# Moving the K products of a state-space gradient kernel behind the next chunk's Z groups, and a fourth staging buffer in its last dense block

## The chip, the cores and the metric

The kernel runs on one core of one Trainium2 chip. It is one launch: inputs and outputs lie in the device's main memory, and the time is that of the launch on the device, in microseconds (us). Five engines work side by side, each with its own queue of instructions that it takes in order: PE (TensorE, matrix products and transposes), DVE (VectorE, elementwise), ACT (ScalarE, copies and functions), POOL (GpSimd) and SP (SyncE), the last two used here almost only to issue DMAs. ACT issues DMAs too. A profile names a wait by the engine that ended it.

## The reference

The kernel computes a forward pass and all its gradients. The forward mixes two branches of the same input x (2048 positions, 448 channels) by a gate per position; branch a is a diagonal state-space convolution with 256 states per channel, branch b a dense layer with squared ReLU.

```python
def _A_ref(u, A_re, A_im, B_re, B_im, C_re, C_im, log_dt, Dskip):
    dt = jnp.exp(log_dt)[:, None]
    A = A_re + 1j * A_im
    Bc = B_re + 1j * B_im
    Cc = C_re + 1j * C_im
    logdA = dt * A
    dB = dt * Bc
    l = (lambda x, dt: x.astype(dt))(jnp.arange(L), A_re.dtype)
    P = jnp.exp(logdA[:, :, None] * l[None, None, :])
    K = jnp.einsum("dn,dnl,dn->dl", Cc, P, dB).real
    ...
    Yf = Uf * Kf[None, :, :, :]                    # convolution of u with K by FFT
    y = irfft2(Yf)[:, :, 0, :L]
    return y.transpose(0, 2, 1) + u * Dskip[None, None, :]

def _B_ref(x, w1, b1, w2, b2):
    h = jnp.einsum("bsd,df->bsf", x, w1) + b1
    r = jnp.where(h > 0, h, 0)
    return jnp.einsum("bsf,fd->bsd", r * r, w2) + b2

g = _sigmoid((x * gate_w).sum(-1, keepdims=True))
out = g * a + (1 - g) * b
_out, _vjp = jax.vjp(_f, ...)                      # then the gradients of all inputs
```

The positions l are rounded to the inputs' type, so that above 256 several positions share one value: the convolution kernel K needs only some of its rows.

## The kernel before

The work has four stretches. First inputs are loaded, their transforms are made (fwd1, fwd2) and powers of the roots exp(dt A) are stored in rec_d. Then comes the **chunk loop** over 14 chunks of 32 channels, with the **dense stages** of branch b beside it. Then the row of K values is read back as xs and transformed, multiplied with the stored spectra (product), and turned back (inv1, inv2). Last come the weight gradients (grad_w2, grad_w1, lines 1218 to 1254).

*The chunk loop.* A chunk c needs two tables per state and channel: X, with 13 of the powers at coarse steps, and Y, with 64 at fine steps. DVE builds them by repeated doubling: x_pair makes the X tables of two chunks at even c (step_x, lines 762 to 767), build_y makes a chunk's Y table in two halves (double, lines 774, 775, 777). ACT supplies the roots for it: expand_x (lines 804, 805) and expand_y (lines 809, 811). From the tables follow:

- kgen(c), line 841: the K values of the chunk, 128 small matmuls (64 x 16 each) of Y with X into the PSUM bank X; k_out (line 849) copies them out, and for chunks 9 and 13 stores the K rows gathered since the last store to k_d (line 855);
- tables_t, lines 867 and 868: X turned by PE, also through bank X, copied by ACT;
- load_yt, line 887: Y turned by a DMA on SP; for the last of four groups turn_yt does it by PE and ACT (lines 879, 880), through bank X;
- back_z(c-1), lines 910 and 914: a Z group is 32 small matmuls of turned Y with the gradient rows dk, into bank F; ACT copies it. Groups 0 and 1 make z01, groups 2 and 3 z23;
- back_p(c-1), lines 930 and 939: DVE multiplies Z with the turned X (called P here, two instructions of 2048 columns per half), and PE sums the products with the matrix sel;
- dk_chunk, lines 892 and 893: ACT lays out the gradient rows.

In the source, iteration c makes back_z and back_p of chunk c-1 around the build of chunk c; kgen(c) stands behind the second half of build_y(c). Y lies in two buffers by the parity of c.

*The dense stages.* hidden (608, 611, ACT 613 and 615) makes the ReLU of a block of 512 positions; project (matmuls 1080, copy 1081, store to br_d 1082) makes 128-position tiles of the dense output, and with w = 1 of the gradient with respect to x; row_block (matmuls 1143 and 1146, ACT 1148, DVE 1155, store 1156) makes the gradient of the hidden values from r, which ACT loads (1129). row_block(3) is the last block and stands behind fwd1 of the K transform in the source. project takes its staging buffers br in turn, three of them, one per tile of the block.

*What sets the order.* The source's order isn't that of the engines. When the program is built, the framework's scheduler fixes each engine's queue by dependencies, buffers and its own estimate, so that the matmuls of the dense stages stand in PE's queue between those of the chunk loop, and the dense product 1155 between DVE's doublings. An issue_after makes one instruction stand behind another. A PSUM bank is reused when the last reader has released it; bank X is shared by kgen, tables_t and turn_yt.

*After the loop.* xs is filled from k_d by 18 DMAs: 11 from SP and 7 from ACT (line 1172, alternating by the first column of a run of equal positions; and line 1175). PE transforms it in fwd1 (line 231, evacuated in lines 208 and 209), the result goes through gd to fwd2 (line 259). grad_w2 then loads rT_d (line 1218) into the memory that held the weights of project, and turns it (line 1223).

Of the kernel before, what the change touches and what calls it, by code (L numbers as in the profile page):

```python
# [338 lines left out]
def kernel(ctx, tc, A_u, A_A_re, A_A_im, A_B_re, A_B_im, A_C_re, A_C_im, A_log_dt, A_Dskip,  # L339
# [487 lines left out]
                              PIY[:, k, ws].rearrange("p w t d -> p (w t) d"), rows=rows)  # L827
        return last

    def kgen(c):  # L830
        ps = K.ps("X", [P, 16 * NA])
        for i in range(CW):
            for gg in range(2):
                for jt in range(2):
                    g = 2 * jt + gg
                    ch = 8 * gg + i
                    k = 0
                    for h in range(2):
                        w = g * 16 + h * 8 + i
                        for t in range(2):  # L840
                            T_.matmul(ps[64 * jt:64 * jt + 64, ch * NA:ch * NA + NA], lhsT=Ys[c % 2][:, w, t, :], rhs=XWs[c % 2][:, 1 - t, w, :, 1],  # L841
                                      start=(k == 0), stop=(k == 3), tile_position=(0, 64 * jt))
                            k += 1
        return ps

    def k_out(c, ps):
        cp, cc = c // GC, c % GC
        kv = KS[:, :, cp].rearrange("p a (g q i) -> p q a g i", g=2, q=GC)[:, cc]
        S.copy(kv, ps[:].rearrange("p (g i a) -> p a g i", g=2, a=NA)[:, 0:VA])
        if c in (9, NCH - 1):  # L850
            c0, c1 = (0, 5) if c == 9 else (5, 7)
            for jt in range(2):
                for (a0, na, st_) in ((0, 2, 1), (2, 2, 2), (4, 2, 1), (6, 6, 256), (12, 1, 1)):
                    nb_ = 1 if a0 == 12 else 64
                    (nc.scalar if jt and c > 9 else G_).dma_start(bass.AP(tensor=k_d, offset=AOFF[a0] * D + 224 * jt + 32 * c0, ap=[[4 * D, nb_], [st_ * D, na], [1, 32 * (c1 - c0)]]),
                                 KS[64 * jt:64 * jt + nb_, a0:a0 + na, c0:c1].rearrange("p a c e -> p a (c e)"))

    def tables_t(c, gp):
        nonlocal xi
        XT = XTr[xi % 4].rearrange("p (t g n) -> p t g n", g=2, t=2)  # L860
        xi += 1
        pt = K.ps("X", [P, 4, 256], bf16)
        for t in range(2):
            for gg in range(2):
                for h in range(2):
                    w = (2 * gp + gg) * 16 + h * 8
                    T_.transpose(pt[:, 2 * t + gg, h * P:(h + 1) * P], XWs[c % 2][:, t, w:w + 8, :, 0].rearrange("p w a -> p (w a)"), ident[:])
        S.copy(XT.rearrange("p t g n -> p (t g n)"), pt[:].rearrange("p a n -> p (a n)"))  # L868
        return XT
# [22 lines left out]
        S.copy(DKs[:, c % 2, 0, :, :, 0:VA], src)  # L892
        S.activation(DKs[:, c % 2, 1, :, :, 0:VA], src, ACT.Copy, scale=brow[:, 0:1])

    def back_z(c, YTs, gs):

        nonlocal zi
        cc = c % GC
        DKc = DKs[:, c % 2]
        zb = Zr[zi % 2].rearrange("p (s t g n) -> p s t g n", t=2, s=2, g=2)  # L900
        zi += 1
        for gg, g in enumerate(gs):
            psz = K.psF()
            for s in range(2):
                for par in (1, 0):
                    for ii in range(4):
                        i = 2 * ii + par
                        m = (1 + par) * NA
                        for t in range(2):
                            T_.matmul(psz[32 * ii:32 * ii + m, t, 256 * s:256 * s + 256],  # L910
                                      lhsT=DKc[64 * t:64 * t + 64, s, g, 2 * ii:2 * ii + 1 + par].rearrange("p i a -> p (i a)"),
                                      rhs=YTs[g][64 * t:64 * t + 64, :, i, :], start=True, stop=True, tile_position=(64 * t, 32 * ii),
                                      skip_group_check=True)
            S.copy(zb[:, :, :, gg].rearrange("p s t n -> p t s n"), psz[:].rearrange("p t (s n) -> p t s n", s=2))  # L914
        return zb

    def back_p(c, XT, zb, gs, after):
# [102 lines left out]
    for c in range(NCH + 1):  # L1020
        z01 = z23 = None
        if c == 0:
            x_next(0)
        elif c % 2 == 1 and c < NCH:
            XTs[c] = [tables_t(c, 0)]
        if 0 < c < NCH:
            YTs[c] = []
        if c > 0:
            z01 = back_z(c - 1, YTs[c - 1], (0, 1))
        if c % 2 == 1 and c < NCH:  # L1030
            XTs[c].append(tables_t(c, 1))
        if c > 0:
            z23 = back_z(c - 1, YTs[c - 1], (2, 3))
        ap = None
        for half in range(2):
            if c < NCH:
                if c > 0:
                    ay = build_y(c, half, ap or ay)
                if half == 1:
                    k_out(c, kgen(c))  # L1040
                for g in (2 * half, 2 * half + 1) if c > 0 else ():
                    YTs[c].append(turn_yt(c, g) if g == 3 or c == NCH - 1 else load_yt(c, g))
                if c + 1 < NCH:
                    if half == 0:
                        lry = load_ry(c + 1)
                        lry1 = lry if c == 0 else lry1
                        if c % 2 == 1:
                            expand_x(c + 1)
                            expand_x(c + 2)
                        if c == 0:  # L1050
                            expand_y(1, 0, 4)
                    elif c == 0:
                        expand_y(1, 4, 5)
                    else:
                        expand_y(c + 1)
                if half == 0:
                    dk_chunk(c)
            ap = None
            if c > 0:
                ap = back_p(c - 1, XTs[c - 1][half], (z01, z23)[half], (2 * half, 2 * half + 1), ay if c < NCH else None)  # L1060
            if half == 0 and c > 0 and c % 2 == 0 and c < NCH:
                ap = x_pair(c, ap)
                x_next(c)
        if c == 0:
            for jp in range(6):
                hidden(0, jp, NT[4:6], ring)
# [3 lines left out]
    def project(lb, w, hblk, ws, brs, banks=NT[0:3]):  # L1070
        nonlocal ni
        for tt in range(4):
            t = 4 * lb + tt
            br = brs[tt % len(brs)]
            ps = K.ps(banks[ni % 3], [P, 512])
            ni += 1
            if w == 0:
                T_.matmul(ps[:, 0:D], lhsT=ones_r[:], rhs=b2row[:], start=True, stop=False)
            for j in range(FT):
                lastm = T_.matmul(ps[:, 0:D], lhsT=hblk[j][:, P * tt:P * tt + P], rhs=ws[:, j, :], start=(w == 1 and j == 0), stop=(j == FT - 1))  # L1080
            S.copy(br, ps[:, 0:D])
            G_.dma_start(bass.AP(tensor=br_d, offset=(t * P * 2 + w) * D, ap=[[2 * D, P], [1, D]]), br)
        return lastm
# [49 lines left out]
    def row_block(lb, banks):  # L1133
        nonlocal ni
        for jp in range(FT // 2):
            pss = []
            i = lb * (FT // 2) + jp
            for j in (2 * jp, 2 * jp + 1):
                ps = K.ps(banks[ni % 3], [P, 512])
                ni += 1  # L1140
                pss.append(ps)
                for dt in range(DT - 1):
                    T_.matmul(ps[:], lhsT=w2Tw[:, jp, dt, j % 2], rhs=dblk[:, dt], start=(dt == 0), stop=False, skip_group_check=True)  # L1143
            for k in range(2):
                h = slice(64 * k, 64 * k + 64)
                T_.matmul(pss[k][:], lhsT=w2Tw[h, jp, 3, k], rhs=dblk[h, 3], start=False, stop=True, tile_position=(64 * k, 0), skip_group_check=True)
            for k in range(2):
                ev = S.mul(hblk[:, 2 * jp + k], pss[k][:], 2.0)

            if i + NR - 3 < 2 * FT:  # L1150
                rq.append(load_r(i + NR - 3))
            for p_ in ([jp - 2] if jp > 1 else []) + ([jp - 1, jp] if jp == FT // 2 - 1 else []):
                hb = hblk[:, 2 * p_:2 * p_ + 2]
                with tc.issue_after(ev.ins):
                    V.tensor_tensor(out=hb, in0=hb, in1=rq[i - jp + p_], op=ALU.mult)  # L1155
                G_.dma_start(bass.AP(tensor=dhT_d, offset=2 * p_ * P * L + 512 * lb, ap=[[L, P], [P * L, 2], [1, 512]]), hb)  # L1156
        if lb < 3:
            load_db(lb + 1)
        return project(lb, 1, [hblk[:, j] for j in range(FT)], w1T, [SB[:, 9344 + 448 * k:9792 + 448 * k] for k in range(3)], banks)
    for lb in range(3):  # L1160
        row_block(lb, NT[0:3])

# [361 lines left out]
```

## Time and profile before

| | us |
|---|---|
| median of 5 runs | 928.09 |
| lowest and highest | 923.62, 934.65 |
| the profiled execution, its time | 929.5 |
| its span in the profile | 927.5 |
| busy in the span: PE, PE weight loads | 716.3, 344.3 |
| DVE, ACT, POOL | 639.7, 592.6, 204.1 |
| mean granted PE clock in the span | 0.836 |

The profile cuts the span in 40 slices of 23.2 us and gives for each the busy share of an engine in tenths (9 is 90% or more). Groups of instructions are named by line, engine and operation; a timeline lists instructions by start and length, and in brackets the idle time of the engine before one and who ended it. "Issue" there means idle time without a wait that the profile shows. The chunk loop runs from about 240 to 604 us.

### The profile page before, as it was taken

The page shows a single profiled execution, that of the slowest core. Times are in us where ns is not written, and L with a number is a line of the kernel's source. Part 1 is how long each engine was busy: PE and PEld are TensorE (multiplying, and loading weights), DVE is VectorE, ACT ScalarE, POOL GpSimd, SP SyncE. Part 2 cuts the span into 40 slices and gives each one's busy share as a digit, 9 for nine tenths or more (in the row PEclk, how much of TensorE's full clock was granted, in tenths as well). Part 3 has the DMA queues.
Part 4 walks back from the last instruction along what each step waited for, and adds up shares of the span by engine and source line. Part 5 has one row for each costly group of instructions (what it writes and reads, how often), then busy time and mean ns, then how long its engine had stood idle before and what let it go on. Part 6 is the DMA issues. An engine that isn't in the chain of part 4 may idle for free.

```text
span 927.5 us, 18872 instructions
## 1 busy us (share of the span) xinstructions
PE 716.3 (77%) x7600; PEld 344.3 (37%) x7633; DVE 639.7 (69%) x1034; ACT 592.6 (64%) x939; POOL 204.1 (22%) x352
## 2 busy tenths in 40 slices
PE   1867745567877887988897879789859869989795
PEld 0333221233434443343563544443323225533253
DVE  4775957694499989989897889834228949659100
ACT  2978768547969877797867746563425545555443
POOL 2341010103112121121221302232213013353120
PEclk9877566577997997997958779999968779989999
DMA  9797675895634746557465576369998988689772
GB/s 234 209 332 275 245 290 222 300 309 147 165 95 103 153 111 136 126 117 171 116 125 141 150 132 178 77 155 296 330 396 270 280 238 263 202 226 268 175 159 62
DMA packets 168238, 184.96 MB, mean 199 GB/s; under 512 B 95347, under 2 KB 145944, under 8 KB 167352
## 3 DMA queue, kind: packets, MB, share of 16 engines
q1 hardware_dynamic: 119062, 83.32, 36.7%
q0 software_dynamic: 21568, 67.46, 22.2%
q10 hardware_dynamic: 27522, 33.00, 11.1%
q8 instruction: 59, 0.97, 0.5%
q14 instruction: 27, 0.22, 0.1%
HBM read 89.60 MB, written 73.13 MB: 175 GB/s over the span
## 4 chain that ended last, share of the span: by engine, by line
PE 31%; ACT 21%; DMA 18%; issue 17%; DVE 9%; POOL 3%; ACTq 1%; POOLq 0%; DVEq 0%; SPq 0%
PE psN L1080 4%; PE psF L1229 3%; DMA S<-rT_d 2%; DMA R<-Y 2%; PE psF L910 2%; PE psX L841 2%; DMA P<-hd 2%; PE psX L879 2%; PE psN L1229 2%; PE psN L296 2%; DMA R<-K 2%; ACT R L868 1%; PE psN L608 1%; DMA rec_d<-F 1%; ACT R L914 1%
## 5 line engine op out<-in xcount | busy, mean ns | idle before, releaser
L914 ACT CAST R<-psF 128x1024 bf16<-128x1024 f32 x56 | 57.6, 1028 | 28.1 <-PE psF L910 28.0
L930 DVE TENSOR_TENSOR P<-R 128x2048 bf16<-128x2048 bf16 x42 | 49.4, 1219 | 28.8 <-ACT R L914 28.8
L1229 PEld LDWEIGHTS <-S 128*128 128x128 bf16 x448 | 42.3, 102 | 54.9 <-issue 15.0
L1229 PE MATMUL psF<-U,S 128*128 128x448 bf16 x224 | 53.2, 385 | 2.8 <-ACT S L1224 2.8
L1080 PE MATMUL psN<-D,S 128*128 128x448 bf16 x208 | 50.2, 377 | 0.5 <-ACT S L618 0.5
L910 PE MATMUL psF<-R,S 64*16 64x256 bf16 (+1 forms) x1344 | 36.7, 308 | 17.2 <-DMA R<-Y 9.4
L608 PE MATMUL psN<-S,U 128*128 128x512 bf16 x115 | 39.2, 428 | 11.3 <-ACT M L613 6.4
L774 DVE TENSOR_TENSOR K<-K,F 128x2048 bf16<-128x2048 bf16 (+3 forms) x42 | 36.4, 866 | 9.4 <-ACT F L809 8.2
L775 DVE TENSOR_TENSOR F<-K,F 128x2048 bf16<-128x2048 bf16 (+3 forms) x42 | 36.0, 856 | 6.8 <-ACT F L811 6.8
L314 PE MATMUL psN<-P,cb_MI 64*128 64x448 bf16 x128 | 30.8, 434 | 12.2 <-ACT st L208 8.2
L1156 POOL DMA_DIRECT2D dhT_d<-D x28 | 20.5, 730 | 89.4 <-DVE D L1155 82.0
L1080 PE MATMUL psN<-S,D 128*128 128x448 bf16 x168 | 38.2, 370 | 2.6 <-DVE D L1155 2.3
L209 DVE CAST K<-psN 128x448 bf16<-128x448 f32 x36 | 21.7, 620 | 26.6 <-PE psN L259 24.5
L774 DVE TENSOR_TENSOR Y<-Y,F 128x2048 bf16<-128x2048 bf16 (+3 forms) x42 | 36.4, 866 | 5.2 <-ACT F L809 3.7
L880 ACT COPY M<-psX 128x1024 bf16<-128x1024 bf16 x27 | 27.6, 1023 | 16.1 <-PE psX L879 13.9
L775 DVE TENSOR_TENSOR F<-Y,F 128x2048 bf16<-128x2048 bf16 (+3 forms) x42 | 36.0, 858 | 2.5 <-ACT F L811 2.5
L1143 PE MATMUL psN<-S,U 128*128 128x512 bf16 x114 | 33.0, 391 | 5.7 <-ACT U L1116 2.2
L777 DVE TENSOR_TENSOR Y<-Y,F 128x2048 bf16<-128x2048 bf16 (+3 forms) x42 | 36.4, 866 | 1.4
L777 DVE TENSOR_TENSOR K<-K,F 128x2048 bf16<-128x2048 bf16 (+3 forms) x42 | 36.3, 865 | 1.4
L910 PEld LDWEIGHTS <-S 64*32 64x32 bf16 (+1 forms) x1792 | 21.9, 92 | 40.5 <-issue 21.9
L1080 PEld LDWEIGHTS <-D 128*128 128x128 bf16 x240 | 22.3, 100 | 26.8 <-issue 5.8
L939 PE MATMUL psS<-P,cb_sel 128*32 128x256 bf16 x224 | 28.9, 325 | 3.9 <-DVE P L930 2.3
(409 smaller groups left out, 1953.5 us busy)
## 6 DMA issues: line engine op xcount, KB each, us to landing
sp<-K ACTq DMA_DIRECT2D x8, 896.0 KB, 4.0
hd<-st ACTq DMA_DIRECT2D x16, 448.0 KB, 4.7
dhT_d<-D POOLq DMA_DIRECT2D x28, 256.0 KB, 5.1
R<-sp SPq DMA_DIRECT2D x8, 896.0 KB, 21.8
S<-rT_d POOLq DMA_DIRECT2D x14, 512.0 KB, 6.5
R<-hd SPq DMA_DIRECT2D x16, 448.0 KB, 9.2
rT_d<-M POOLq DMA_DIRECT2D x18, 256.0 KB, 3.8
rec_d<-F POOLq DMA_DIRECT2D x2, 1920.0 KB, 9.8
```

The lines of the kernel that those rows point to most:

```text
L314: nc.tensor.matmul(ps[kk2][:, 0:D], lhsT=MI[r0:r0 + 64, ri, :], rhs=sp[r0:r0 + 64, 2 * q2 + ii, ri, :], start=(ri == 0), stop=(ri == 1), t ...
L608: T_.matmul(ps[:], lhsT=w1w[:, dt, j * P:j * P + P], rhs=ub[:, dt], start=(dt == 0), stop=False, skip_group_check=True)
L774: V.tensor_tensor(out=hi, in0=lo, in1=bcast_dims(pr, [0, (None, n // 2), 1]), op=ALU.mult)
L775: V.tensor_tensor(out=Vv.rearrange("p (x a q) -> p x a q", x=rows, q=2), in0=lo, in1=bcast_dims(pi, [0, (None, n // 2), 1]), op=ALU.mult)
L777: return V.tensor_tensor(out=T4[:, :, :, n:2 * n], in0=T4[:, :, :, n:2 * n], in1=V4, op=ALU.add)
L910: T_.matmul(psz[32 * ii:32 * ii + m, t, 256 * s:256 * s + 256], lhsT=DKc[64 * t:64 * t + 64, s, g, 2 * ii:2 * ii + 1 + par].rearrange("p i ...
L914: S.copy(zb[:, :, :, gg].rearrange("p s t n -> p t s n"), psz[:].rearrange("p t (s n) -> p t s n", s=2))
L930: lastp = V.tensor_tensor(out=pr.rearrange("p s t g n -> p s t (g n)"), in0=zv, in1=(xb if r == 0 else rev_dim(xb, 2)), op=ALU.mult)
L939: T_.matmul(sps[s][32 * gr:32 * gr + 32, r, :], lhsT=sel[:, k, off:off + 32], rhs=Q[r][:, s, t, gg, :], start=(g < 2 and cc == 0 and t == ...
L1080: lastm = T_.matmul(ps[:, 0:D], lhsT=hblk[j][:, P * tt:P * tt + P], rhs=ws[:, j, :], start=(w == 1 and j == 0), stop=(j == FT - 1))
L1143: T_.matmul(ps[:], lhsT=w2Tw[:, jp, dt, j % 2], rhs=dblk[:, dt], start=(dt == 0), stop=False, skip_group_check=True)
L1229: lastm = T_.matmul(ps[:, 0:width], lhsT=hh[:, t, :], rhs=(DB2[:, t, :] if w == 0 else U[:, t, 0:D + 1]), start=(t == 0), stop=(t == LT - 1))
```

## The change

kgen gets its bank from the caller and makes the matmuls of channels i0 to i1 only. For chunks 1 to 12 it is no longer called in the chunk's own iteration but inside back_z of the next one: behind each of the four Z groups a quarter (even chunks), or behind groups 0 and 1 a half each (odd chunks, whose X table is rewritten in the next iteration). k_out follows behind z23 or z01. Bank X is taken for it before the first Z group, so both turned X tables of an odd chunk are made before that. Chunks 0 and 13 stay as they were. In the last dense block, project gets a fourth staging buffer.

```diff
-    def kgen(c):
-        ps = K.ps("X", [P, 16 * NA])
-        for i in range(CW):
+    def kgen(c, ps, i0=0, i1=CW):
+        for i in range(i0, i1):
...
-        return ps
+        return lastk
...
-    def back_z(c, YTs, gs):
+    def back_z(c, YTs, gs, kps=None):
...
             S.copy(zb[:, :, :, gg].rearrange("p s t n -> p t s n"), psz[:].rearrange("p t (s n) -> p t s n", s=2))
+            if kps is not None:
+                with tc.issue_after(lastz.ins):
+                    if c % 2 == 0:
+                        kgen(c, kps, 2 * g, 2 * g + 2)
+                    elif g < 2:
+                        kgen(c, kps, 4 * g, 4 * g + 4)
...
         elif c % 2 == 1 and c < NCH:
-            XTs[c] = [tables_t(c, 0)]
+            XTs[c] = [tables_t(c, gp) for gp in range(2)]
         if 0 < c < NCH:
             YTs[c] = []
         if c > 0:
-            z01 = back_z(c - 1, YTs[c - 1], (0, 1))
-        if c % 2 == 1 and c < NCH:
-            XTs[c].append(tables_t(c, 1))
-        if c > 0:
-            z23 = back_z(c - 1, YTs[c - 1], (2, 3))
+            kps = K.ps("X", [P, 16 * NA]) if 1 < c < NCH else None
+            z01 = back_z(c - 1, YTs[c - 1], (0, 1), kps)
+            if kps is not None and c % 2 == 0:
+                k_out(c - 1, kps)
+            z23 = back_z(c - 1, YTs[c - 1], (2, 3), kps)
+            if kps is not None and c % 2 == 1:
+                k_out(c - 1, kps)
...
-                if half == 1:
-                    k_out(c, kgen(c))
+                if half == 1 and c in (0, NCH - 1):
+                    kps = K.ps("X", [P, 16 * NA])
+                    kgen(c, kps)
+                    k_out(c, kps)
...
-        return project(lb, 1, [hblk[:, j] for j in range(FT)], w1T, [SB[:, 9344 + 448 * k:9792 + 448 * k] for k in range(3)], banks)
+        return project(lb, 1, [hblk[:, j] for j in range(FT)], w1T, [SB[:, o_:o_ + 448] for o_ in (9344, 9792, 10240, 10752)[0:3 if lb < 3 else 4]], banks)
```

## The prediction

> **What bounds the kernel now.** I read the page's forty slices first, then DVE's groups and the timeline of the chunk loop (240 to 604 us), then what follows it. The slices:
>
> ```profile
> PE   1867745567877887988897879789859869989795
> DVE  4775957694499989989897889834228949659100
> DMA  9797675895634746557465576369998988689772
> ```
>
> One slice is 23.2 us. From slice 11 to 25 DVE stands at eight to nine tenths, so in the chunk loop it sets the pace. From slice 26 on PE is mostly at eight to nine tenths (with dips to five) and DMA is nearly full from 27 to 31. So a change to the loop is worth what it takes out of DVE's idle time, and after it the question is when PE's remaining work can run.
>
> Between 250 and 600 us DVE idles 26.1 us in gaps over 0.25 us: 9.9 us in front of L774 and L775, which wait for the expanded roots from ACT (L809, L811); 2.7 us before P (L930); 13.5 us before the dense product L1155. The last two kinds, in the timeline (bracket: idle time before, and its releaser):
>
> ```profile
> 484.26 2.36 DVE L930 TENSOR_TENSOR P<-R 128x2048 bf16<-128x2048 bf16 x2 [0.85 <-ACT R L914]
> ...
> 494.29 0.69 DVE L1155 TENSOR_TENSOR D<-D,M 128x1024 bf16<-128x1024 bf16 x1 [5.93 <-ACT D L1148]
> ...
> 551.59 2.36 DVE L930 TENSOR_TENSOR P<-R 128x2048 bf16<-128x2048 bf16 x2 [1.87 <-ACT R L914]
> ...
> 558.66 0.69 DVE L1155 TENSOR_TENSOR D<-D,S 128x1024 bf16<-128x1024 bf16 x1 [4.30 <-ACT D L1148]
> ```
>
> Everywhere else P starts well after its Z copy (L914) has ended: by 13 to 30 us or 4 to 10 us, except chunks 5, 9 and 11, first half: 1.6, 0.03 and 0.03 us. In these the K burst stands between the first and the second Z group.
>
> **Part 1a, the burst leaves that place.** No instruction is added or removed; 128 K matmuls per chunk move for chunks 1 to 12. Before, an odd chunk's burst looks like this:
>
> ```profile
> 361.51 2.16 PE L841 MATMUL psX<-X,K 128*64 128x16 bf16 x123
> ...
> 366.44 0.17 PE L841 MATMUL psX<-X,K 128*64 128x16 bf16 x1 [2.77 <-issue]
> ```
>
> 2.2 us of work, and a hole of 2.77 us without a wait, with an instruction fetch of 16 KB starting in it at 363.92. The Trainium skill (Runtime: NRT & Kernel Launch, Instruction fetch mechanics) has PE refilled in blocks of 256 instructions, and crossing one mostly hidden. The burst with its weight loads is exactly 256. By the rule the burst delays the second group by 2.2 us; by the row by up to 5 us, and at 541.97 by 3.6. The row decides. In the new order the burst comes in two runs of 64, of 96 and 32, or whole (chunks 5 and 11), because a piece also waits until the X bank is free. In chunk 11 it falls wholly behind the second group, in chunk 9 half. Either way the 0.85 and 1.87 us go: **-2.7 us** (ends 0 and -2.7). Late next is L930's own place behind build_y, so no more is won. For even chunks P has over 4 us of slack; moving K there is free. The last K piece must end before the Y block is rewritten, which also stands behind P. With K moves k_out: 0.34 us on ACT, past Y turns and Z copies that now come first, and for chunk 9 ten k_d stores on POOL (0.6 us each, 6 us). POOL is busy 22% of the span, its other stores in the loop wait for ACT and DVE, and these k_d rows are first read at 607: free, and at worst 6 us for a br_d store nobody needs before 621.
>
> A rule that speaks against pieces: the same skill (Perfetto Trace Analysis, Matmul Optimizations) wants matmuls back to back in batches, since PE's power follows its use. A burst split and run at half clock would add, as an estimate, 2.2 us per chunk, 26 us of PE in all. In the row, 64 K matmuls would take 1.1 us with Z groups of 32 (0.63 us) right beside them, and PE is at seven to nine tenths anyway. I cost it at nothing.
>
> **Part 1b, ACT's order.** At the starts of chunks 5, 7 and 9 the new order has 21 projections before the X transposes instead of 23, 26 and 25; 11 x 0.2 us = -2.2. At the start of chunk 2 both Y copies (L880, 1.02 us) now stand before L809 and L811: +2.0; at chunk 3 one L615 (1.07 us, 0.45 slack): +0.6. Both X tables of odd chunks are now made together, since K holds the bank; P needs the second only 16 us later. Together **+0.4** (ends -2 and +3).
>
> **Part 1c, the dense product in DVE's queue.** The first L1155 waited 5.93 us. On its chain ACT idled 2.54 us for k_out (L849) behind a K burst, then 1.99 and 1.16 for the Y turns behind k_out. In the new order the same copies stand there, with the Y turns first; I count them through to a product at about 493 instead of 494.3: -1.3. The three of chunk 11's first half (0.77, 0.95, 1.56) move behind a P pair: -1.9 of 3.3. At 558.66 two products that stood among the first X steps now stand seven steps later, about 7 us, so the 4.30 go. Sum **-7.5** (ends 0 and -13.5; the trace doesn't show the new order, and the last item is the surest).
>
> Loop: -2.7 + 0.4 - 7.5 = -9.8 us.
>
> **Part 1d, what comes late.** DVE's loop is faster, so less dense work fits beside it. When the last K burst (chunk 13, not moved) ends, PE has issued 336 projections (L1080) and 87 row-block matmuls (L1143) before, 315 and 84 after. Both must reach 392 and 126 before the K transform (L231) can run but for its first matmul. Before:
>
> ```profile
> 602.35 2.21 PE L841 MATMUL psX<-X,K 128*64 128x16 bf16 x128
> ...
> 626.96 2.44 PE L1080 MATMUL psN<-S,D 128*128 128x448 bf16 x12
> ...
> 631.58 0.31 ACTq L1172 DMA_DIRECT2D X<-k_d  x1
> ...
> 639.38 0.73 PE L231 MATMUL psN<-X,cb_F1BD 128*128 128x448 bf16 x3
> ```
>
> From 604.6 to 639.4 is 34.8 us. In the new order one L231 (j = 3) stands before the last 21 row-block matmuls and all 56 projections, and waits for the X load that ACT issues fourth (16 rows): before at 631.58. A new head-of-line wait: all of PE stands behind it, DVE's copy of it (L209) stands before five L1155. ACT now reaches this load after 4 L880, 3 L914, 2 L1081, 3 L1148 and five k_d issues, 13.4 us of its own; the third L914 ended 14.4 us after the burst. So issue at +16.3, landing 4.7 later: +21. Then 21 row-block matmuls (6 to 9 us, take 7.5) and 56 projections (11.2 to 12.4, take 11.8): +40.3, against 34.8: **+5.5** (ends 0 and +16.2). From there on the order of all engines is that of before, with PE or DMA full, so the delay reaches the end.
>
> **Part 2, the fourth buffer.** The fourth copy (L1081) of the last block waits for the first br_d store:
>
> ```profile
> 682.96 0.53 ACT L1081 CAST S<-psF 128x448 bf16<-128x448 f32 x1 [8.98 <-DMA br_d<-S]
> 683.98 1.33 PE L259 MATMUL psN<-K,M 128*64 128x448 bf16 x6 [7.04 <-ACT K L208]
> ...
> 688.32 0.29 PE L1223 MATMUL psX<-ident,S 128*128 128x128 bf16 x1 [3.02 <-DMA S<-rT_d]
> ```
>
> It looks like 7 us. But after 14 of L259, PE's next is the transpose L1223, whose rT_d load was issued at 674.80 and lands at 688.3 whatever ACT does: its buffer is freed by PE's last projection. PE would stand there from about 679. **0** (ends 0 and -3).
>
> **Sum:** -9.8 + 5.5 + 0 = -4.3 us. The profiled run took 929.5 us (span 927.5); the median of the runs shown is 928.09. So about 925 by the profile, 924 by the median.
>
> **Rivals.** *Gain kept* (0.22): the 24 missing matmuls fit PE's 3.8 idle us of 606 to 627 and the early L231 finds its load landed: -9.8, 918. For: PE isn't full there; against: ACT's queue before the load. *Early L231 holds PE* (0.18): the load lands as late after the burst as before, at +31.7, not +21; then +16.2 - 9.8 = +6.4, 934.5. It decides from +25.3 us on, where gain and loss cancel. For: these loads wait on ACT behind copies and cost 2.9 and 3.2 us before; against: in the new order the first stand before most L1148. *DVE's waits stay* (0.15): L1155 still waits its 13.5 us; -2.7 + 0.4 + 5.5, 931. *Forecast* 0.45. That the pieces aren't where the words say is true for chunks 5 and 11, and costs nothing by 1a.
>
> **Numbers.** A measurement of this kernel tells about 1%, 9.3 us. The faster side is most of *gain kept*; the slower the far part of the early L231: 0.22, 0.65, 0.13. The range reaches from 913 (a loop nearer -15) to 937 (L231 late).
>
> **What would show it.** Right: no idle time at P of chunks 9 and 11; at most 4 us before L1155 until 600; the last K burst some 10 us earlier; the bulk of L231 40 us after it; L1081 without a wait, and PE before L1223 waiting about 9 us instead. Wrong: the last K burst less than 5 us earlier, L231 more than 25 us after it, or the first L1223 much nearer to L259.

## The result, and the profile after

The changed kernel took 924.76 us (median of 43 runs, 914.45 to 935.34) beside 927.59 us of the kernel before (80 runs): ratio **0.9973, 95% interval 0.9955 to 0.9991**. That is 2.5 us less by the ratio, where the forecast said 4.3. Measured again later on: 0.9941 (0.9905 to 0.9977). A ratio is taken over the executions within 1.5% of a kernel's fastest; where few of them are, the quotient of the medians of all executions is given beside it.

One caution for every profile below: the three profiled executions of the changed order (929.4, 929.7 and 932.5 us) all lie above their kernel's median, by 4.7 to 8.8 us, so they tell which waits there are and where, and the ratios tell what the change is worth. The first of them, 929.42 us, took as long as the profiled execution of before (929.5); these two are compared stretch by stretch.

The slices of the changed kernel, in the rows that were shown of before:

```profile
PE   1876744657887978798899779889858869998895
DVE  4675857596388999999897997932417967859300
DMA  9797675896542757437556485558999988789762
```

DVE still stands at seven to nine tenths from slice 11 to 25 (counted from 0, as in the prediction; before had a seven among these too, in slice 21), so it still sets the loop's pace, and PE and DMA are still full behind it. The picture is that of before; the change lies in single waits. In the timeline of DVE (P is L935 now, the dense product L1164, the root doublings still L774 and L775):

```profile
456.68 0.40 DVE L774 TENSOR_TENSOR K<-K,F 128x256 bf16<-128x256 bf16 x1 [1.34 <-ACT F L809]
...
459.13 0.38 DVE L775 TENSOR_TENSOR F<-K,F 128x256 bf16<-128x256 bf16 x1 [2.05 <-ACT F L811]
...
492.41 2.35 DVE L935 TENSOR_TENSOR P<-R 128x2048 bf16<-128x2048 bf16 x2
...
503.45 0.69 DVE L1164 TENSOR_TENSOR D<-D,M 128x1024 bf16<-128x1024 bf16 x1 [6.22 <-ACT D L1157]
...
554.37 2.35 DVE L935 TENSOR_TENSOR P<-R 128x2048 bf16<-128x2048 bf16 x2
...
569.47 0.69 DVE L1164 TENSOR_TENSOR D<-D,S 128x1024 bf16<-128x1024 bf16 x1 [4.94 <-ACT D L1157]
```

The two P of chunks 9 and 11 have no bracket any more: they don't wait, as forecast. (Another P, at 478.68, waits 1.16 us for PE.) The two long waits of the dense product are there as before (5.93 and 4.30 then), and the waits for the roots have grown: two of twelve stand in the first rows.

Behind the loop (K is L840 now, projections L1089, the load of X L1181):

```profile
602.88 2.22 PE L840 MATMUL psX<-X,K 128*64 128x16 bf16 x128
...
619.87 1.74 ACTq L1181 DMA_DIRECT2D X<-k_d  x1
...
627.34 0.36 PE L231 MATMUL psN<-X,cb_F1BD 128*128 128x448 bf16 x1
...
637.52 8.50 PE L1089 MATMUL psN<-S,D 128*128 128x448 bf16 x44 [0.56 <-DVE D L1164]
...
645.85 0.73 PE L231 MATMUL psN<-X,cb_F1BD 128*128 128x448 bf16 x3
```

The early matmul of the transform runs at 627.34 without a wait: PE got to it 22.2 us after the K burst's end, 605.1. The fourth load that ACT issues left 14.8 us after it. From the burst to the bulk it is 40.7 us; 40.3 were forecast.

At the fourth buffer (the second transform L259, the first transpose of grad_w2 now L1232):

```profile
683.16 0.81 PE L259 MATMUL psN<-K,M 128*64 128x448 bf16 x6 [0.24 <-ACT K L208]
...
694.52 0.29 PE L1232 MATMUL psX<-ident,S 128*128 128x128 bf16 x1 [10.55 <-DMA S<-rT_d]
```

The wait of 7.04 us before L259 is 0.24 now, and PE waits 10.55 us before the transpose, where it waited 3.02: for the load of rT_d. Nothing is won.

Over the two executions of equal length, from the first P to the last K burst: 361.8 us before, 358.2 after (-3.6, forecast -9.8). From there to the bulk of the transform: 34.8 and 40.7 (+5.9, forecast +5.5). From the bulk to the first transpose: 48.9 and 48.7. The rest is code that the change leaves as it was, and differs by 4.2 us ahead of the first P and by -6.4 from the transpose on. So this pair alone shows the changed stretches 2.0 us slower; it cannot carry a gain of 2.5 us, and the parts had to be measured by themselves.

### The profile page after: what moved, and what is told of

Read it like the earlier page. It is cut to its first block, busy times and chain, and to the rows that moved or that the text cites. A ratio compares the mean times of both kernels' runs of the same rounds, so it can differ in the third digit from the quotient of the medians.

```text
span 927.3 us, 18876 instructions
## 1 busy us (share of the span) xinstructions
PE 726.5 (78%) x7602; PEld 347.5 (37%) x7633; DVE 639.3 (69%) x1034; ACT 593.6 (64%) x939; POOL 204.1 (22%) x352
## 4 chain that ended last, share of the span: by engine, by line
PE 34%; ACT 21%; DMA 17%; issue 17%; DVE 7%; POOL 3%; ACTq 1%; POOLq 0%; DVEq 0%
PE psN L1089 5%; PE psF L1238 3%; DMA R<-Y 3%; PE psX L840 3%; DMA S<-rT_d 2%; ACT R L913 2%; PE psF L909 2%; ACT M L879 2%; PE psN L608 2%; DMA P<-hd 2%; PE psN L1238 2%; PE psN L1152 1%; DMA rec_d<-F 1%; ACT F L811 1%; ACT F L809 1%
## 5 line engine op out<-in xcount | busy, mean ns | idle before, releaser
L935 DVE TENSOR_TENSOR P<-R 128x2048 bf16<-128x2048 bf16 x42 | 49.5, 1219 | 24.6 <-ACT R L913 23.4
L1238 PEld LDWEIGHTS <-S 128*128 128x128 bf16 x448 | 42.3, 102 | 54.9 <-issue 14.9
L909 PE MATMUL psF<-R,S 64*32 64x256 bf16 (+1 forms) x1344 | 35.9, 303 | 21.0 <-DMA R<-Y 12.2
L1089 PE MATMUL psN<-D,S 128*128 128x448 bf16 x208 | 51.8, 383 | 0.0
L608 PE MATMUL psN<-S,U 128*128 128x512 bf16 x116 | 38.8, 434 | 4.3 <-issue 1.5
L774 DVE TENSOR_TENSOR K<-K,F 128x2048 bf16<-128x2048 bf16 (+3 forms) x42 | 36.3, 865 | 8.0 <-ACT F L809 6.7
L775 DVE TENSOR_TENSOR F<-K,F 128x2048 bf16<-128x2048 bf16 (+3 forms) x42 | 36.0, 856 | 7.5 <-ACT F L811 7.5
L774 DVE TENSOR_TENSOR Y<-Y,F 128x2048 bf16<-128x2048 bf16 (+3 forms) x42 | 36.4, 866 | 6.8 <-ACT F L809 5.6
L1152 PE MATMUL psN<-S,U 128*128 128x512 bf16 x115 | 36.2, 413 | 5.8 <-ACT D L1157 2.9
L209 DVE CAST K<-psN 128x448 bf16<-128x448 f32 x36 | 21.6, 621 | 27.0 <-PE psN L259 25.1
L775 DVE TENSOR_TENSOR F<-Y,F 128x2048 bf16<-128x2048 bf16 (+3 forms) x42 | 36.0, 856 | 5.3 <-ACT F L811 5.3
L1089 PE MATMUL psN<-S,D 128*128 128x448 bf16 x168 | 37.5, 366 | 0.7 <-DVE D L1164 0.6
L909 PEld LDWEIGHTS <-S 64*16 64x16 bf16 (+1 forms) x1792 | 21.8, 91 | 42.7 <-issue 18.7
L1232 PEld LDWEIGHTS <-S 128*128 128x128 bf16 x376 | 24.5, 101 | 22.8 <-DMA S<-rT_d 11.4
L1157 ACT ACTIVATE D<-psN 128x512 bf16<-128x512 f32 x42 | 23.2, 601 | 14.3 <-PE psN L1155 12.6
L1089 PEld LDWEIGHTS <-D 128*128 128x128 bf16 x240 | 22.6, 100 | 24.8 <-issue 5.5
## 6 DMA issues: line engine op xcount, KB each, us to landing
rec_d<-F POOLq DMA_DIRECT2D x2, 1920.0 KB, 10.2
```

The lines of the kernel that those rows point to most:

```text
L608: T_.matmul(ps[:], lhsT=w1w[:, dt, j * P:j * P + P], rhs=ub[:, dt], start=(dt == 0), stop=False, skip_group_check=True)
L774: V.tensor_tensor(out=hi, in0=lo, in1=bcast_dims(pr, [0, (None, n // 2), 1]), op=ALU.mult)
L775: V.tensor_tensor(out=Vv.rearrange("p (x a q) -> p x a q", x=rows, q=2), in0=lo, in1=bcast_dims(pi, [0, (None, n // 2), 1]), op=ALU.mult)
L909: lastz = T_.matmul(psz[32 * ii:32 * ii + m, t, 256 * s:256 * s + 256], lhsT=DKc[64 * t:64 * t + 64, s, g, 2 * ii:2 * ii + 1 + par].rearra ...
L935: lastp = V.tensor_tensor(out=pr.rearrange("p s t g n -> p s t (g n)"), in0=zv, in1=(xb if r == 0 else rev_dim(xb, 2)), op=ALU.mult)
L1238: lastm = T_.matmul(ps[:, 0:width], lhsT=hh[:, t, :], rhs=(DB2[:, t, :] if w == 0 else U[:, t, 0:D + 1]), start=(t == 0), stop=(t == LT - 1))
```

## The experiments

The table is worked out from the timelines: DVE's idle time in gaps over 0.25 us between the first P and the last K burst, by what waited; "loop" is that stretch, "to bulk" the way from the last K burst to the bulk of L231. Each ratio is against before on the same chip. The quotients of the medians lie within 0.0025 of the ratios, except for k_part_only (0.997), late_dense (1.002) and whole_k_late (0.984).

| kernel | ratio (95%) | profiled, us | loop | DVE idle: roots, dense, all | to bulk |
|---|---|---|---|---|---|
| before | | 929.5 | 361.8 | 9.9, 13.5, 26.2 | 34.8 |
| before_again | 1.0007 (0.9975-1.004) | 925.9 | 363.6 | 10.8, 14.2, 27.4 | 32.7 |
| buffer_only | 1.0018 (0.9993-1.0043) | 928.9 | 363.6 | 11.2, 14.0, 28.0 | 33.5 |
| after | 0.9973 (0.9955-0.9991) | 929.4 | 358.2 | 13.5, 11.7, 26.4 | 40.7 |
| after_again | 0.9941 (0.9905-0.9977) | 929.7 | 364.8 | 8.8, 16.4, 32.2 | 39.4 |
| k_part_only | see below | 932.5 | 361.9 | 16.1, 13.7, 29.8 | 38.9 |
| late_dense | 0.995 (0.9914-0.9986), see below | 926.1 | 355.7 | 10.3, 10.1, 21.6 | 39.1 |
| only_9_11 | 0.9974 (0.9948-1.0001) | 918.9 | 352.6 | 3.8, 11.9, 16.7 | 34.5 |
| not_9_11 | 1.0005 (0.9978-1.0032) | 926.3 | 360.0 | 9.1, 12.6, 24.7 | 36.8 |
| whole_burst | 0.9885 (0.9851-0.9919) | 920.3 | 348.8 | 7.2, 8.8, 17.5 | 39.4 |
| whole_again | 0.9897 (0.9862-0.9932) | 912.1 | 346.0 | 5.5, 8.5, 14.9 | 38.8 |
| whole_k_late | 0.9895 (0.9845-0.9945) | 919.5 | 349.7 | 9.1, 8.5, 18.3 | 39.2 |
| halves_early | 0.9957 (0.9931-0.9984) | 911.2 | 345.5 | 7.6, 6.5, 14.2 | 38.6 |
| whole_pinned | 0.9869 (0.9831-0.9907) | 918.2 | 349.7 | 9.0, 9.3, 18.2 | 39.7 |

### The two parts, and both kernels once more

k_part_only takes the buffer out of the changed kernel, buffer_only puts it into the kernel before:

```diff
-[SB[:, o_:o_ + 448] for o_ in (9344, 9792, 10240, 10752)[0:3 if lb < 3 else 4]]
+[SB[:, 9344 + 448 * k:9792 + 448 * k] for k in range(3)]
```

> The K part of the change with the three staging buffers of before; every engine's order is that of the changed kernel. Theory A (the fourth buffer gives nothing, as the prediction costed it): the same ratio as the changed kernel, 0.9973 of before, and from the first transpose of grad_w2 to the end the time of the changed kernel's profile, 226.7 us. Theory B (the gain comes from the fourth buffer, behind the loop): ratio 1.000, a little over, and 232.9 us from that transpose to the end as in before. Both: the first P to the end of the last K burst 358 us (before 361.8), the last K burst to the bulk of the transform's matmuls 40.7 us (before 34.8).

> The fourth staging buffer of the last dense block alone on the kernel before; every engine's order is that of before. Theory A (it gives nothing: the next load waits anyway): 1.000; the fourth copy without its wait of 8.98 us, and PE waiting about 9 us before the first transpose of grad_w2 in place of 7.04 before the second transform. Theory B (it gives the whole gain): 0.9973, and the end 3 to 6 us nearer to the first transpose of grad_w2.

> The changed kernel once more, for a second profile of it beside the parts: 0.997 by its earlier runs. If the stretches of its first profile are its own and not that execution's: first P to last K burst 358 us, last K burst to the bulk of the transform 40.7, first transpose of grad_w2 to the end 226.7.

> The kernel before against itself: 1.000, its distance from 1 shows what such a comparison can tell. Its second profile shows how far one stretch differs between two executions of the same program: if the stretches are the program's own, first P to last K burst 361.8 us, last K burst to the bulk of the transform 34.8, first transpose of grad_w2 to the end 232.9.

The K part alone had a median of 923.67 us beside 926.44 of before, a quotient of 0.997. (The ratio computed for it, 0.9865 with 0.9822 to 0.9908, rests on 6 of its 22 executions, those next to its fastest, 906.69 us, and isn't used.) The buffer alone: 1.0018, with 1 inside the interval. So the gain is the K part's, as far as differences of this size can tell, and theory B, my own after the first profile, fell. The stretch on which it stood, from the first transpose to the last instruction of an engine, is no property of a program: 232.9 and 225.0 us in the two executions of before, 226.7 and 221.7 in those of after. In buffer_only PE waits before the transpose as in the changed kernel:

```profile
693.38 0.29 PE L1223 MATMUL psX<-ident,S 128*128 128x128 bf16 x1 [9.44 <-DMA S<-rT_d]
```

"Last K burst to bulk" on the other hand is the program's own: 32.7 to 34.8 us in the three executions of the old order, 38.9 to 40.7 in the three of the new one.

The second profile of the changed kernel has a wait that the prediction did not think of. DVE timeline, then PE:

```profile
561.84 0.29 DVE L784 COPY X<-st 128x512 bf16<-128x512 bf16 x1 [4.42 <-PE psX L840]
...
558.96 2.84 PE L840 MATMUL psX<-X,K 128*64 128x16 bf16 x128
```

The X table of an odd chunk is rewritten in the next iteration, and K of chunk 11 still read it: the new place has a late edge too, which in the first profile was missed by 2 us (the burst ended at 555.0, this copy began at 556.85).

### Which chunks

In only_9_11 and not_9_11 K is moved for chunks 9 and 11 alone, or for all of the change's chunks but these:

```diff
-            kps = K.ps("X", [P, 16 * NA]) if 1 < c < NCH else None
+            kps = K.ps("X", [P, 16 * NA]) if 1 < c < NCH and (c - 1) in (9, 11) else None
...
-                if half == 1 and c in (0, NCH - 1):
+                if half == 1 and not (0 < c < NCH - 1 and c in (9, 11)):
```

> The K products moved for chunks 9 and 11 alone (both turned X tables early for all odd chunks; this alone leaves every order as it was), and the fourth buffer. The two stalls of the P instructions of chunks 9 and 11 (0.85 and 1.87 us before, 0.8 and 1.6 to 2.0 in two more profiles) go. Theory A (step 1a: these stalls are the loop's share of the gain): the whole gain of the changed kernel, 0.997. Theory B (the gain comes from the other chunks): 1.000. No early matmul of the transform stands in PE's queue in this order, so the last K burst to its bulk takes the 33 to 35 us of before.

> The K products moved for all the chunks of the change except 9 and 11, with the fourth buffer. The counterpart of the run for chunks 9 and 11. Theory A (the P stalls of chunks 9 and 11 are the gain): 1.000, with both stalls as before. Theory B (the other chunks bring it): 0.997. No early matmul of the transform stands in PE's queue here either.

Chunks 9 and 11 alone give 0.9974, the other ten 1.0005. The intervals overlap, so this is no proof, but it points to 9 and 11. That the P stalls are what these two chunks give isn't shown either: over its 22 executions only_9_11 had a mean granted clock of 0.8375, before beside it 0.8315, and at 4 us for 0.01 (last section) this alone would make 2.4 us, the whole gain. By what way the new order comes to more clock was not tested. Half of the expectation missed: not_9_11 has no stall at P of chunks 9 and 11 either, since other instructions moved with K, and in its place P waits 0.8 to 1.3 us at three other chunks for PE. Both orders have no early L231, and both are short on the way to the bulk, but not equally: only_9_11, with 336 projections and 87 row-block matmuls issued before the last burst as in before, 34.5 us; not_9_11 with 327 and 84, 36.8; the changed order with 315 and 84, 38.9 to 40.7. The way follows the dense work that is left.

### The wait of the dense product

late_dense puts the first product of two row blocks behind the last X step of chunks 10 and 12:

```diff
-    rx_, ry_ = {}, {}
+    rx_, ry_, xl = {}, {}, {}
...
+                xl[c] = ap
...
-                with tc.issue_after(ev.ins):
+                with tc.issue_after(ev.ins if p_ or lb > 1 else xl[10 + 2 * lb].ins):
```

> The changed kernel with the first dense product of the first and of the second row block made to stand behind the last X step of chunks 10 and 12 on DVE, instead of among the X steps, where three profiles of the changed kernel show it waiting 6.2 to 9.6 us and 4.9, 6.7 and 3.6 us. Theory A (these waits are DVE time that the loop could have, as step 1c took it): both go, the last K burst comes 8 to 14 us earlier, and the kernel is 5 to 10 us faster than the changed one, ratio 0.987 to 0.992 of before. Theory B (PE is the one that is late there, and what the loop saves is given back while PE works off the dense products behind the loop): the waits go or are smaller, the last K burst comes earlier, the bulk of the transform after it comes later by as much, and the ratio stays at 0.996 to 0.998.

In place of the first products, the next ones now wait, 3.63 and 1.89 us:

```profile
503.97 0.69 DVE L1165 TENSOR_TENSOR D<-D,M 128x1024 bf16<-128x1024 bf16 x1 [3.63 <-ACT D L1158]
...
563.60 0.69 DVE L1165 TENSOR_TENSOR D<-D,U 128x1024 bf16<-128x1024 bf16 x1 [1.89 <-ACT D L1158]
```

Four others wait 0.5 to 1.7 us each: 10.1 us in all instead of 11.7 to 16.4. The ratio, 0.995, rests on 10 of its 22 executions; the median of all, 928.3 us, is above the 926.2 of before, a quotient of 1.002. The 5 to 10 us of theory A didn't come, and the way to the bulk stayed at 39.1 us, so that theory B, which had it grow, isn't confirmed either. What holds is that taking this wait from DVE's queue is worth nothing measurable.

### The pieces

whole_burst issues the 128 K products of each chunk in one piece, behind the second Z group; whole_again is the same kernel once more; whole_k_late puts the copy of even chunks back behind the fourth group.

```diff
                 with tc.issue_after(lastz.ins):
-                    if c % 2 == 0:
-                        kgen(c, kps, 2 * g, 2 * g + 2)
-                    elif g < 2:
-                        kgen(c, kps, 4 * g, 4 * g + 4)
+                    if g == 1:
+                        kgen(c, kps)
...
-            if kps is not None and c % 2 == 0:
+            if kps is not None:
                 k_out(c - 1, kps)
             z23 = back_z(c - 1, YTs[c - 1], (2, 3), kps)
-            if kps is not None and c % 2 == 1:
-                k_out(c - 1, kps)
```

> The changed kernel with each chunk's K products in one piece behind the second Z group of the next chunk (k_out behind it for all chunks), instead of four or two pieces. Theory A (the pieces cost and bring nothing, as step 1a took it): the ratio of the changed kernel, 0.994 to 0.997, within 2 us. Theory B (the pieces are what helps, since a whole burst of 128 holds the third Z group up): 1.000, with stalls of the second half's P by 1 to 3 us. Theory C (pieces cost PE time at a low clock, as the rule on back-to-back batches says): 3 to 20 us faster than the changed kernel.

> The kernel with each chunk's K products in one piece (whole_burst) once more, for a second profile and to see whether its gain holds. Theory A (it does): ratio 0.985 to 0.992 of before, first P to last K burst 347 to 352 us, DVE's idle time in the loop near 17 us. Theory B (the first measurement was a lucky one): the ratio of the changed kernel, 0.994 to 0.997, and DVE idle 26 to 32 us.

> whole_burst with the copy of the K products (k_out) of even chunks put back to where the changed kernel has it, behind the fourth Z group; PE has the order of whole_burst. It separates the two things in which whole_burst differs from the changed kernel. Theory A (the pieces on PE are what costs): as whole_burst, 0.985 to 0.992. Theory B (the later k_out on ACT, which holds bank X, is what costs): as the changed kernel, 0.994 to 0.997.

0.9885, 0.9897 and 0.9895 (the last from 6 runs): about 10 us under before, and some 4 to 8 under the changed kernel (0.9941 and 0.9973). So the number of theory C, which I had put last, came in (its reason, the clock, is weighed below), and the gain isn't k_out's. halves_early keeps the halves of the odd chunks, while its even chunks come out whole (k_out as in whole_burst):

```diff
-                    if c % 2 == 0:
-                        kgen(c, kps, 2 * g, 2 * g + 2)
-                    elif g < 2:
+                    if g < 2:
                         kgen(c, kps, 4 * g, 4 * g + 4)
```

> The changed kernel with two halves behind Z groups 0 and 1 for even chunks too, k_out behind group 1. In the order that results the even chunks' K products are one run of 128, the odd chunks' (1, 3, 7 and 9) two runs of 64 with 21 or 32 Z matmuls between them as in the changed kernel, and k_out stands where whole_burst has it. Theory A1 (the even chunks' runs of 96 and 32 cost): as whole_burst, 0.985 to 0.992. Theory A2 (the odd chunks' halves cost, since a half stands ahead of the rest of the second Z group): as the changed kernel, 0.994 to 0.997. If both do, halfway.

0.9957, the changed kernel's ratio, about 0.0067 or 6 us above whole bursts (0.9957 less 0.989; on the one chip where these ran together its median was 920.9 us, theirs 911.9 to 915.0). What the runs of 96 and 32 of even chunks cost can't be told from zero. The 6 us go with the odd chunks' halves, but the halves alone are not shown to be their cause: the scheduler placed other instructions differently too. Between whole_burst and halves_early the first five dense products stand at other places in DVE's queue, and some 38 projections in PE's. No run keeps all the rest in place and splits the bursts alone.

Nor does a profile show where the time goes. In whole_again the second of the long dense waits is shorter (L1160 there); over the four profiles with whole bursts it is at most 2.6 us, against 3.6 to 6.7 in those of the changed order. But in the one profile of halves_early it is 1.65 us, and the loop (345.5 us) and DVE's idle time (14.2 us) are as short there as with whole bursts; that execution was the fastest of its 22 (911.2 us). Whole_again:

```profile
489.07 0.69 DVE L1160 TENSOR_TENSOR D<-D,M 128x1024 bf16<-128x1024 bf16 x1 [4.71 <-ACT D L1153]
...
554.42 0.69 DVE L1160 TENSOR_TENSOR D<-D,S 128x1024 bf16<-128x1024 bf16 x1 [2.60 <-ACT D L1153]
```

A second thing that differs is PE's clock at chunk 4. Its K products in the first profile of the changed kernel, and in whole_again:

```profile
353.22 2.74 PE L840 MATMUL psX<-X,Y 128*64 128x16 bf16 x96
...
356.44 1.05 PE L840 MATMUL psX<-X,Y 128*64 128x16 bf16 x32
```

```profile
349.07 2.21 PE L840 MATMUL psX<-X,Y 128*64 128x16 bf16 x128 [0.41 <-ACT P L867]
```

From start to start within a run, such a matmul takes 26.9, 23.6 and 24.0 ns in the three profiles of the changed order and 26.7 in halves_early, but 16.0 in all four with whole bursts. The table by stretch of the changed kernel shows the clock behind it (busy time of PE, PE weight loads, DVE, ACT and POOL, each with its number of instructions; then the granted clock, DMA share and GB/s):

```profile
348.50:351.90 3.40, 1.53 (x34) 1.14 (x18) 3.30 (x5) 3.40 (x6) 3.04 (x6) 1.00 0.37 106
351.90:355.30 3.40, 3.00 (x99) 2.60 (x99) 3.33 (x4) 3.40 (x6) 1.29 (x4) 0.53 0.20 57
355.30:358.70 3.40, 3.18 (x73) 1.93 (x70) 3.37 (x4) 2.28 (x4) 0.41 (x1) 0.50 0.22 79
358.70:362.10 3.40, 3.40 (x10) 0.92 (x9) 3.40 (x4) 1.85 (x3) 0.73 (x1) 0.50 0.87 167
362.10:365.50 3.40, 3.40 (x36) 1.19 (x43) 3.37 (x4) 2.66 (x4) 0.73 (x1) 0.97 1.12 199
```

PE was busy 1.53 of 3.40 us (first number), then ran 10 us at half clock. The odd chunk's halves come one chunk earlier; that they leave PE this emptier stretch is argued, not shown. By clock alone the 6 us can't be explained: whole bursts at other chunks ran at half clock too (1, 2, 10 and 11 in whole_burst), and over all runs the mean granted clock was 0.829 to 0.830 in the changed order and 0.831 to 0.839 with whole bursts, which at 4 us for 0.01 (last section) makes 0.4 to 4 us. By what way the order with halves costs the 6 us stays open.

### The early matmul of the transform

whole_pinned is whole_burst with fwd1 of the transform behind the third row block:

```diff
-        row_block(lb, NT[0:3])
+        lastrb = row_block(lb, NT[0:3])
...
-    K.fwd1(lambda j: xv[:, j], gd[2], stage= ...)
+    with tc.issue_after(lastrb.ins):
+        K.fwd1(lambda j: xv[:, j], gd[2], stage= ...)
```

> whole_burst with the whole of the K transform's fwd1 behind the last projection of the third row block on PE, so that no early matmul of it stands in the queue; the loop keeps its order. Theory A (the early matmul costs nothing by itself, since its load has landed when PE gets there; the longer way from the last K burst to the bulk of the transform is the dense work that PE hadn't done before): that way stays at 38 to 41 us and the ratio is that of whole_again. Theory B (the early matmul is what makes it longer): it falls to 33 to 36 us and the kernel is 3 to 5 us faster than whole_again.

```profile
594.02 2.22 PE L840 MATMUL psX<-X,K 128*64 128x16 bf16 x128
...
627.61 8.50 PE L1085 MATMUL psN<-S,D 128*128 128x448 bf16 x44 [0.29 <-DVE D L1160]
...
635.94 0.73 PE L231 MATMUL psN<-X,cb_F1BD 128*128 128x448 bf16 x3
```

No L231 stands ahead of the projections (L1085 here), and the way is 39.7 us, as with it. Theory A holds: the early matmul costs nothing; what the way follows is the dense work that is left. The ratio, 0.9869, has an interval that holds those of whole_burst and whole_again; this version and those beat both kernels, and are not told apart from each other.

## Why the prediction was right or wrong

**The total** came out near the forecast: -2.5 us by the first ratio and -5.5 by the second, against -4.3. Its terms did not, so that the agreement is in good part luck: the largest, 1c, gave nothing that can be seen, and with the pieces, which were put at nothing, go some 6 us.

**1a, the burst leaves its place: right, and one term of it wrong.** The P stalls of chunks 9 and 11 are gone (-2.7), and these chunks alone measured 0.9974, 2.4 us, though not_9_11 and the clock of only_9_11 leave room for another vehicle. Part of the wait came back elsewhere: over the three profiles of each order P waited 2.4 to 2.8 us in all before, and 1.2, 2.5 and 0 after, nearly all of it for PE at other chunks. The step that failed is the one where the rule on back-to-back batches was weighed against the row and costed at nothing: the versions with whole bursts are some 6 us faster. I had estimated the rule's price at 26 us, 2.2 us for each chunk at half clock. In the traces a burst of 128 takes 3.6 us at half clock and 2.2 at full, which is 1.4 us more, so the same sum gives an estimate of 17 us; the 6 us are a third of that, go with the odd chunks' halves, and may in part be other instructions that moved with them. The row I set against it (64 K matmuls in 1.1 us) was true at full clock only. That nothing is queued behind the moved products held in two of three profiles; in the third, L784 waited 4.42 us.

**1b, ACT's order: mis-sized in the pair, else not settled.** +0.4 us forecast; the waits for the roots went from 9.9 to 13.5 us in the pair of equal executions, +3.6. Over three profiles of each order they were 9.9 to 11.2 before and 8.8 to 16.1 after, a mean of +2.2 us with a spread that holds the forecast.

**1c, the dense product: failed.** -7.5 us forecast, and -1.8 in that pair; over the three profiles of each order the mean is 13.9 us before and 13.9 after. The two long waits, 10.2 us of the 13.5, stayed at 11.2. What failed is the path. The prediction counted ACT's copies through to a product at "about 493 instead of 494.3", and in before ACT did set it: it came to the copy without a wait (L1148, first two rows). In the changed kernel it has to wait for PE (L1157, last two rows):

```profile
493.02 1.23 ACT L1148 ACTIVATE D<-psN 128x512 bf16<-128x512 f32 x2
...
557.53 1.09 ACT L1148 ACTIVATE D<-psN 128x512 bf16<-128x512 f32 x2
```

```profile
502.82 0.60 ACT L1157 ACTIVATE D<-psN 128x512 bf16<-128x512 f32 x1 [2.01 <-PE psN L1155]
...
567.33 0.60 ACT L1157 ACTIVATE D<-psN 128x512 bf16<-128x512 f32 x1 [1.69 <-PE psN L1155]
```

So PE's row-block matmul comes last there, and moving the product itself (late_dense) brought nothing. "The last item is the surest" was the worst: of 4.30 us, 4.94 were left.

**1d, what comes late: right.** 34.8 to 40.7 us beside a forecast of 34.8 to 40.3, and the runs bear the cause out: with the early matmul pinned away the way stays as it is, and in the orders with more dense work issued before the burst it is shorter. The load was no obstacle; it was issued at +14.8 instead of +16.3. So the rival *early L231 holds PE* is out.

**Part 2, the fourth buffer: right.** 1.0018, and the wait moved to the load of rT_d: 10.55 us, about 9 forecast.

**The sum, then.** By difference, and not seen in any profile, the loop of a typical execution gave 8 to 11 us (2.5 to 5.5, and 5.9 of 1d on top). That is the forecast's 9.8, but not by its terms; in the pair of equal executions the loop gave 3.6, and over three profiles of each order 1.4 on the mean (363.0 to 361.6). Two of the signs for "wrong" that the prediction named did come in the first profile: the last K burst was not earlier (605.1 beside 604.6, by 3.6 us counted from the first P), and before the dense product 11.7 us were left, not 4. *DVE's waits stay* (931) describes these profiles better than the forecast does; the ratios don't bear it out.

## What to carry to other kernels

When a block of small matmuls is moved behind other work, move it whole first, and split it only if a measured wait asks for it: here the move with whole bursts was worth some 10 us, and the version with halves in the odd chunks only about 4. A wait in an engine's queue is worth its length only if what ends it can be earlier; ask which engine made it late (PE, for the dense product) before counting the time as won. Where an effect is a third of a per cent, compare stretches over several profiles, and trust only those that repeat: the 5.9 us behind the loop did, the loop itself and the tail did not.

## What the runs showed of the hardware

The granted clock of PE moves in steps of 3.41 us between full and half. The Trainium skill (TensorE: Matmul & The Clock Gate, Part 1: The HAM clock gate) names this window, and half rate after an idle one. The trace agrees on window and rate, but PE need not be idle: worked out window by window between 240 and 620 us of the changed kernel's first profile, the 15 full-speed windows followed by a half-speed one had PE busy 13 to 69%, and those that led back to full speed 81 to 100%. Before was alike: 0 to 71% and 86 to 100%. No sharp line comes out of it, since in the changed kernel's profile windows after which full speed stayed had PE busy 55 to 100%. In this loop, 102 to 116 us run at half clock in the three profiles of the old order and 116 to 137 in those of the new one, though PE is busy 0.84 of the time from 240 to 600 us.

What that costs is uneven. A small K matmul (64 weight columns, 16 columns moved) takes 16.0 ns at full and 26.8 at half clock, a burst of 128 2.2 or 3.6 us. The 3.6 us of chunk 11 in before, which the prediction put beside the instruction fetch, was half clock; the hole of 2.77 us at 366 in before, with the fetch, came again in the two other profiles of that order (2.1 and 2.2 us). Over the 59 runs of before beside the first four experiments, an execution with 0.01 more of mean clock was 4.0 us shorter (a straight line through clock and time), which is more than the whole effect that was measured here.
